# Attention steps of an HGRN2 and mixture-of-experts kernel: scores and Y in fours, the swapped v on GpSimd, banks allotted once, gate before the state products

## The chip, the cores and the metric

The kernel runs on one core of a Trainium2 chip. The core has five engines with their own instruction streams: TensorE (PE, with weight loads shown as PEld), VectorE (DVE), ScalarE (ACT), GpSimd (POOL) and SyncE (SP), which here issues transfers. They wait for each other by semaphores only. The metric is the time of one execution on the device in microseconds. The kernel before took 455.57 us (median of three runs, 452.97 to 456.45).

## The reference

Two blocks follow each other. The first is a gated linear recurrence for 4 batches and 8 heads, over 768 positions with a head width of 48:

```python
f = 1.0 / (1.0 + np.exp(-f_logit))
for t in range(S):
    state = f[:, :, t, :, None] * state + np.einsum('bhd,bhe->bhde', k[:, :, t], v[:, :, t])
    y[:, :, t] = np.einsum('bhd,bhde->bhe', q[:, :, t], state)
```

Its output, 3072 tokens of 384 values, goes to the second block: logits for 8 experts (`x @ w_gate`), an assignment of the tokens to the experts in order of their logits with at most 384 tokens per expert, and for each expert `max(x @ w1, 0) @ w2` with an inner width of 1024. All is float32.

## The kernel before, in words

**Tiling.** The recurrence is cut into chunks of 128 positions: 6 chunks of each of 4 batches, 24 in all, numbered so that the batch runs fastest. Within a chunk the recurrence becomes matrix products. With decays accumulated from the middle of the chunk (the rows up to 63 and those from 64 on have different signs), k and q are scaled by powers of the decay, and the scores k.q of all pairs of positions are formed, masked to the lower triangle, and multiplied by v. What comes from earlier chunks is added through a state per head, 48x48, which is carried from chunk to chunk of the same batch. The heads are packed in pairs on the partitions: a head's 48 rows are padded to 64, and a pair fills the 128.

**The stages of a chunk**, each a small function that takes a chunk's dictionary `G`:

- `load` and `fetch` (L140, L147): q, k, f and v come in by transfers of 192 KB from SP, f one chunk further ahead.
- `load_turned` (L156): two transfers of 64 KB each copy half of v inside the chip, so that the upper and lower 64 positions of heads 4 to 7 change places. The result is w.
- `clamp` (L162, GpSimd), `decays` (L166, ScalarE: exponential and logarithm), `cumulated` (L171, one matmul of float32, which is two passes on TensorE), `clipped` (L177, VectorE, from that sum's bank L), `powers` (L182, ScalarE: ek and eq), `scaled` (L187: kg on GpSimd, qg on VectorE).
- `turn_q`, `turn_k` and their copies (L229): four transposes each into a bank of PSUM, the accumulation memory of TensorE, and a copy by ScalarE.
- `lengths`, `spanned`, `faded`, `kept_part`, `products`, `next_state` (L201 to L267): the decay over the whole chunk and the state.
- `scores` (L269): 16 matmuls of 64x64 tiles, 128 or 64 columns wide; the array works as four tiles, two for the rows (`par`) and two for the output partitions. `masked0` and `masked1` (L281, VectorE) copy them under the mask out of the two banks A.
- `inner` (L300): 16 matmuls of masked scores with v (heads 0 to 3) and w (heads 4 to 7) into the two banks Y; `outer` (L314): 8 with the state.
- `joined` (L325): ScalarE copies one bank Y and VectorE adds the other. `turn_y`, `copy_y` (L331, L337) turn the sum to tokens in rows; `gate` (L344) forms the logits from it in 16 weight loads, into columns of bank L beside the decay sums; `gated`, `with_logits`, `store` (L353 to L361) put x and its logits into a table in HBM.

**The order.** Nothing is scheduled by a program: `tc.manual_schedule` (L611) keeps the order in which the Python code issues. `attention` (L386) runs through steps; in each it first issues `load_turned` and `load`, and then the tuple `stages` (L364), where each entry names a stage and how many chunks behind the step it works: (`scores`, 1) at step 10 is chunk 9. So every engine has a fixed order within a step, and several chunks are in work at once. `begun`, `drain` and `finale` are the orders of the first and last steps, and (None, 0) marks where small extra work (`later`, L380) goes, mainly on VectorE: tables for the second block, and from L573 the first choices of experts.

**Banks.** PSUM has eight banks: one L, two T (turns), two A, two Y and one small. A and Y are allotted once (L110). L is allotted anew in each step (`room[0] = L`, L172), and T anew for each turn of q, k and y in rotation (L231, L332), so three turns per step pass over two banks.

After the attention part come the counting and sorting of the assignment (L732 on) and the experts (`ffn`, L653), whose two large matmul lines are L674 and L688.

## Time and profile before

| what | value |
|---|---|
| median of three runs | 455.57 us |
| profiled execution, its own time | 453.23 us |
| span from first to last instruction | 451.4 us |
| mean granted TensorE clock | 0.978 |
| TensorE busy | 423.5 us, 94% |
| VectorE / ScalarE / GpSimd busy | 186.8 / 151.6 / 117.2 us |
| matmuls of the scores (L276), busy | 21.8 us with 128, 20.0 us with 64 columns |
| gate (L350) with mean of one | 13.0 us in the steps, 203 ns |
| SP issues of w (L159) | 48, 64 KB each, 2.6 us to landing |
| packets of the transfer queue | 119,664, 52.11 MB |

An instruction's line is that of the kernel's text, and a name such as `qg` is the tile that it writes or reads. "Idle before" is the time in which the engine had nothing to do ahead of an instruction, with what ended it. TensorE's matmuls are pipelined, so their durations overlap: the distance between starts tells more. The attention part reaches to about 157 us, the counting and sorting to about 178 us, and the experts to the end.

### The profile page before, as it was taken

How to read it: one execution, taken by the hardware profiler on the slowest of the kernel's cores; microseconds unless marked ns; L12 is line 12 of the kernel's file. 1: busy time of each engine (PE TensorE's matmuls, PEld its weight loads, DVE VectorE, ACT ScalarE, POOL GpSimd, SP SyncE). 2: the span in 40 equal slices, each digit the busy share in tenths (PEclk: the TensorE clock that was granted, in tenths of full speed). 3: DMA queues.
4: the chain of work that ended last, by engine and by line, in shares of the span. 5: the costliest groups of instructions: out<-in, count | busy, mean ns of one | idle time of the engine just before them, and what ended most of it. 6: DMA issues, size and time to landing. Idle time of an engine off the chain costs nothing.

```text
span 451.4 us, 11287 instructions
## 1 busy us (share of the span) xinstructions
PE 423.5 (94%) x4743; PEld 311.8 (69%) x4743; DVE 186.8 (41%) x600; ACT 151.6 (34%) x350; POOL 117.2 (26%) x182
## 2 busy tenths in 40 slices
PE   7789999999999768999999999999999999999991
PEld 3678887888787646767686868688887556556550
DVE  5679788777788763176565661000000000000000
ACT  4656565665665201222121213122323212213200
POOL 5344444334444006710100105111013203011010
PEclk9999999999999859999999999999999999999997
DMA  8888887987786792845353003048842201100000
GB/s 163 163 183 193 185 188 169 205 195 176 168 199 158 241 383 61 274 177 184 122 173 143 17 19 108 17 162 298 306 161 65 62 19 49 39 17 36 0 36 22
DMA packets 122987, 62.47 MB, mean 138 GB/s; under 512 B 103088, under 2 KB 117552, under 8 KB 122928
## 3 DMA queue, kind: packets, MB, share of 16 engines
q1 hardware_dynamic: 119664, 52.11, 43.3%
q0 software_dynamic: 3264, 9.56, 6.5%
q8 instruction: 39, 0.64, 0.6%
q14 instruction: 20, 0.16, 0.1%
HBM read 48.91 MB, written 9.54 MB: 129 GB/s over the span
## 4 chain that ended last, share of the span: by engine, by line
PE 65%; issue 13%; DMA 7%; DVE 5%; SPq 3%; ACT 3%; POOL 2%; POOLq 0%; ACTq 0%
PE H L674 22%; PE O L688 21%; DMA f<-in_f_logit_dram 4%; PE T L233 3%; DMA w<-v 3%; PE Y L309 3%; PE A L276 2%; PE nothing L106 2%; SPq L152 2%; PE X L334 2%; PE L L174 2%; PE Y L320 1%; PE small L254 1%; PE Xe L663 1%; POOL out_dram L694 1%
## 5 line engine op out<-in xcount | busy, mean ns | idle before, releaser
L688 PE MATMUL O<-w,hT 128*128 128x384 f32 x384 | 132.6, 490 | 0.0
L674 PE MATMUL H<-xeT,w 128*128 128x256 f32 (+2 forms) x624 | 130.6, 366 | 0.7 <-ACT xeT L666 0.7
L674 PEld LDWEIGHTS H<-xeT,w 128*128 128x128 f32 x624 | 99.1, 191 | 27.1 <-ACT xeT L666 1.0
L688 PEld LDWEIGHTS O<-w,hT 128*128 128x128 f32 x384 | 69.7, 190 | 39.2 <-issue 0.2
L694 POOL DMA_INDIRECT out_dram<-o,tok x24 | 23.5, 977 | 210.7 <-ACT o L693 201.1
L678 ACT ACTIVATE hT<-H 128x256 f32<-128x256 f32 (+2 forms) x104 | 38.2, 368 | 88.3 <-PE H L674 86.4
L693 ACT COPY o<-O 128x384 f32<-128x384 f32 x24 | 11.5, 479 | 74.5 <-PE O L688 73.0
L284 DVE COPY_PREDICATED am<-mask,A 128x512 f32<-128x512 int32 x48 | 34.4, 723 | 0.3 <-PE A L276 0.2
L666 ACT COPY xeT<-Xe 128x384 f32<-128x384 f32 x24 | 11.4, 480 | 61.4 <-PE Xe L663 61.4
L191 POOL TENSOR_TENSOR kg<-k,ek 128x384 f32<-128x384 f32 x24 | 26.1, 1087 | 12.9 <-ACT ek L185 12.6
L727 POOL DMA_INDIRECT xe<-xd,tok x24 | 23.3, 969 | 23.2 <-DMA w<-in_moe_w_dram 16.2
L191 DVE TENSOR_TENSOR qg<-q,eq 128x384 f32<-128x384 f32 x24 | 22.2, 926 | 12.8 <-ACT eq L185 12.7
L328 ACT COPY yT<-Y 128x512 f32<-128x512 f32 x24 | 14.1, 586 | 35.4 <-PE Y L320 31.2
L276 PE MATMUL A<-qT,kT 48*64 48x128 f32 (+1 forms) x768 | 21.8, 251 | 0.0
L309 PE MATMUL Y<-am,w 64*64 64x64 f32 (+1 forms) x384 | 19.6, 247 | 1.7 <-DMA w<-v 1.7
L233 PE MATMUL T<-ident,qg 128*128 128x128 f32 x96 | 15.7, 284 | 5.6 <-DVE qg L191 5.0
L163 POOL TENSOR_SCALAR f<-f 128x384 f32<-128x384 f32 x24 | 12.8, 533 | 31.2 <-DMA f<-in_f_logit_dram 31.2
L174 PE MATMUL L<-g,wcum 128*128 128x384 f32 x48 | 19.8, 494 | 0.6 <-ACT g L169 0.6
L329 DVE TENSOR_TENSOR yT<-Y,yT 128x512 f32<-128x512 f32 x24 | 16.4, 683 | 8.1 <-ACT yT L328 8.0
L309 PE MATMUL Y<-am,v 64*64 64x128 f32 (+1 forms) x384 | 19.5, 247 | 0.1
L276 PEld LDWEIGHTS A<-qT,kT 48*64 48x64 f32 x768 | 18.0, 133 | 0.5
L168 ACT ACTIVATE f<-f 128x384 f32<-128x384 f32 x24 | 12.7, 528 | 16.7 <-POOL f L163 16.7
(203 smaller groups left out, 520.4 us busy)
## 6 DMA issues: line engine op xcount, KB each, us to landing
w<-in_moe_w_dram SPq DMA_DIRECT2D x16, 1536.0 KB, 8.0
xd<-x SPq DMA_DIRECT2D x24, 196.0 KB, 3.6
f<-in_f_logit_dram SPq DMA_DIRECT2D x24, 192.0 KB, 4.1
k<-in_k_dram SPq DMA_DIRECT2D x24, 192.0 KB, 4.0
q<-in_q_dram SPq DMA_DIRECT2D x24, 192.0 KB, 3.8
v<-in_v_dram SPq DMA_DIRECT2D x24, 192.0 KB, 4.2
w<-v SPq DMA_DIRECT2D x48, 64.0 KB, 2.6
xe<-xd,tok POOLq DMA_INDIRECT x24, 3.2
```

What stands on the lines that cost most here:

```text
L174: nc.tensor.matmul(out=G["Lv"], lhsT=wcum[:], rhs=g_bufs[G["i"] % NB][:, :, 0:DH], start=True, stop=True)
L191: eng.tensor_tensor(out=t[:, :, 0:DH], in0=G[src][:], in1=G[e][:], op=ALU.mult)
L233: nc.tensor.transpose(out=T[:, 128 * hp:128 * hp + 128], in_=G[src][:, 2 * hp:2 * hp + 2, :].rearrange("t h d -> t (h d)"), identity=ident[:])
L276: nc.tensor.matmul(out=A[par][to, 128 * hp + first * j:128 * hp + 128], lhsT=G["kT"][rows, hp, HC * j:HC * j + HC], rhs=G["qT"][rows, hp, ...
L284: nc.vector.copy_predicated(am[:, par].rearrange("s (a b) t -> s a b t", b=2), mask[:].unsqueeze(2).to_broadcast((128, 2, 2, 128)), A[par] ...
L309: nc.tensor.matmul(out=G["Y"][r0][DP * r:DP * r + DP, 128 * blk + first:128 * blk + 128], lhsT=v, rhs=G["am"][rows, h % 2, h // 2, first:128],
L329: nc.vector.tensor_tensor(out=flat, in0=G["Y"][0][:], in1=flat, op=ALU.add)
L674: nc.tensor.matmul(out=L["H"][:, 0:w], lhsT=slots[e][0][:, d, 128 * ft:128 * ft + 128], rhs=xT[:, d, 0:w], start=(d == 0), stop=(d == DC - 1))
L678: nc.scalar.activation(out=hT[:, ft, 0:w], in_=L["H"][:, 0:w], func=AF.Relu)
L688: nc.tensor.matmul(out=L["O"][:, 0:D], lhsT=hT[:, ft, 128 * i:128 * i + 128], rhs=slots[e][1][:, ft, :], start=(ft == 0), stop=(ft == FC - 1))
L694: nc.gpsimd.indirect_dma_start(out=outs[next(tiles)][:, :], out_offset=bass.IndirectOffsetOnAxis(ap=token(e, first_block + i), axis=0), in ...
L727: nc.gpsimd.indirect_dma_start(out=t[:], out_offset=None, in_=xd[:, :], in_offset=bass.IndirectOffsetOnAxis(ap=token(e, i), axis=0))
```

## The change

Four parts are changed together.

- In `scores` and `inner` the loops are reordered. Before, the four blocks came in the order 0, 2, 1, 3, each with its wide and narrow matmuls one after the other. Now each run of four matmuls has the same width and goes to the four different tiles.
- `load_turned` becomes the stage `turned`: GpSimd copies the two halves of v itself, 64 partitions by 256 values each. It stands in the order behind `lengths` and ahead of `powers`, for chunk step - 1; in the drain behind `copy_k`. SP issues no transfers for w.
- The banks T and L are allotted once. q and y always use T[0], k uses T[1]; the gate writes `lengthy`. Two small turns of the bounds and the last chunk's `inner` use them too.
- In `stages`, `gate` and `gated` move directly behind `turn_y` and `copy_y`, ahead of `products` and `lengths`; `masked1` moves behind `clipped`; `spanned` and `next_state` move behind `scaled`. Besides, the first choices of experts, which were made in steps 18 and 19 for two columns of chunks each, are made column by column in steps 7 to 21.

```diff
@@ -100,14 +100,15 @@
     v_bufs = [kept([128, H, DP], FP32, f"v{i}") for i in range(NV)]
     wg_rows = kept([128, HP, E], FP32, "wg_rows")
 
-    def idle_turns(n, tag="T"):
-        nothing = ps("nothing", tag)
+    def idle_turns(n, tag=None):
+        nothing = ps("nothing", tag) if tag else T[0]
         for _ in range(n):
             nc.tensor.matmul(out=nothing[:, 0:3 * 128], lhsT=ones16[:], rhs=idle[:], start=True,
                              stop=True)
 
     small = ps("small", "small")
-    A, Y = ([ps(nm, nm) for _ in range(2)] for nm in "AY")
+    lengthy = ps("L", "L")
+    T, A, Y = ([ps(nm, nm) for _ in range(2)] for nm in "TAY")
 
     with tc.manual_schedule(engines=FIXED):
         nc.scalar.preload_act_table_set("natural_log_exp_and_others")
@@ -153,11 +154,11 @@
                 out=t[:, :, 0:DH], in_=src[b, :, C * c:C * c + C, :].rearrange("h t d -> t h d"))
             G[nm] = t
 
-    def load_turned(G):
+    def turned(G):
         G["w"] = w = work.tile([128, H // 2, DP], FP32, name="w", tag="w", bufs=4)
         for z in range(2):
-            nc.sync.dma_start(out=w[HC * z:HC * z + HC],
-                              in_=G["v"][HC - HC * z:C - HC * z, H // 2:H])
+            nc.gpsimd.tensor_copy(out=w[HC * z:HC * z + HC],
+                                  in_=G["v"][HC - HC * z:C - HC * z, H // 2:H])
 
     def clamp(G):
         nc.gpsimd.tensor_scalar(out=G["f"][:], in0=G["f"][:], scalar1=3.0e38, scalar2=-40.0,
@@ -169,8 +170,7 @@
         nc.scalar.activation(out=g[:, :, 0:DH], in_=f[:], func=AF.Ln, bias=1.0, scale=1.0)
 
     def cumulated(G):
-        room[0] = L = ps("L", "L")
-        G["Lv"] = L[:, 0:D].rearrange("t (h d) -> t h d", d=DH)
+        G["Lv"] = lengthy[:, 0:D].rearrange("t (h d) -> t h d", d=DH)
         nc.tensor.matmul(out=G["Lv"], lhsT=wcum[:], rhs=g_bufs[G["i"] % NB][:, :, 0:DH],
                          start=True, stop=True)
 
@@ -228,10 +226,10 @@
 
     def turn_of(nm, src):
         def turn(G):
-            G[nm + "_ps"] = T = ps("T", "T")
+            G[nm + "_ps"] = t = T[nm == "kT"]
             for hp in range(HP):
                 nc.tensor.transpose(
-                    out=T[:, 128 * hp:128 * hp + 128],
+                    out=t[:, 128 * hp:128 * hp + 128],
                     in_=G[src][:, 2 * hp:2 * hp + 2, :].rearrange("t h d -> t (h d)"),
                     identity=ident[:])
 
@@ -268,15 +266,14 @@
 
     def scores(G):
         first = 0 if G["i"] == 0 else HC
-        for hp in ORDER:
-            for j in range(2):
-                to = slice(HC * (j ^ (hp // 2)), HC * (j ^ (hp // 2)) + HC)
-                for par in range(2):
-                    rows = slice(DP * par, DP * par + DH)
-                    nc.tensor.matmul(
-                        out=A[par][to, 128 * hp + first * j:128 * hp + 128],
-                        lhsT=G["kT"][rows, hp, HC * j:HC * j + HC],
-                        rhs=G["qT"][rows, hp, first * j:128], start=True, stop=True)
+        for b, j, a in ((b, j, a) for b in range(2) for j in range(2) for a in range(2)):
+            hp, to = 2 * a + b, slice(HC * (j ^ a), HC * (j ^ a) + HC)
+            for par in range(2):
+                rows = slice(DP * par, DP * par + DH)
+                nc.tensor.matmul(
+                    out=A[par][to, 128 * hp + first * j:128 * hp + 128],
+                    lhsT=G["kT"][rows, hp, HC * j:HC * j + HC],
+                    rhs=G["qT"][rows, hp, first * j:128], start=True, stop=True)
 
     def masked(G, pars=(0, 1)):
         G["am"] = am = a_bufs[G["i"] % NB]
@@ -295,21 +292,18 @@
     def places(blk):
         return [(4 * (blk // 2) + 2 * r + blk % 2, r) for r in range(2)]
 
-    ORDER = [0, 2, 1, 3]
-
     def inner(G):
         last = G is chunks[-1]
-        G["Y"] = [ps("Y", "L"), ps("Y", "T")] if last else Y
-        for blk in ORDER:
-            for r0 in range(2):
-                j = r0 ^ (blk // 2)
-                rows, first = slice(HC * r0, HC * r0 + HC), 0 if last else HC * j
-                for h, r in places(blk):
-                    v = G["v"][rows, h, :] if blk < 2 else G["w"][rows, h - H // 2, :]
-                    nc.tensor.matmul(
-                        out=G["Y"][r0][DP * r:DP * r + DP, 128 * blk + first:128 * blk + 128],
-                        lhsT=v, rhs=G["am"][rows, h % 2, h // 2, first:128],
-                        start=(blk == ORDER[0]), stop=G["R"] is None, skip_group_check=True)
+        G["Y"] = [lengthy, T[1]] if last else Y
+        for b, j, a in ((b, j, a) for b in range(2) for j in range(2) for a in range(2)):
+            blk, r0 = 2 * a + b, j ^ a
+            rows, first = slice(HC * r0, HC * r0 + HC), 0 if last else HC * j
+            for h, r in places(blk):
+                v = G["v"][rows, h, :] if a == 0 else G["w"][rows, h - H // 2, :]
+                nc.tensor.matmul(
+                    out=G["Y"][r0][DP * r:DP * r + DP, 128 * blk + first:128 * blk + 128],
+                    lhsT=v, rhs=G["am"][rows, h % 2, h // 2, first:128],
+                    start=(b == 0 and j == 0), stop=G["R"] is None, skip_group_check=True)
 
     def outer(G):
         if G["R"] is None:
@@ -329,7 +323,7 @@
         nc.vector.tensor_tensor(out=flat, in0=G["Y"][0][:], in1=flat, op=ALU.add)
 
     def turn_y(G):
-        G["X"] = X = ps("X", "T")
+        G["X"] = X = T[0]
         for hp in range(HP):
             nc.tensor.transpose(out=X[:, 128 * hp:128 * hp + 128], in_=G["yT"][:, hp, :],
                                 identity=ident[:])
@@ -343,7 +337,7 @@
 
     def gate(G):
         G["lg"] = r = (part_of(G, 0, E) if G["i"] + 3 >= len(chunks)
-                        else room[0][:, D:D + E])
+                        else lengthy[:, D:D + E])
         for hp in range(HP):
             for j in range(2):
                 half = slice(HC * j, HC * j + HC)
@@ -361,14 +355,14 @@
         nc.sync.dma_start(out=xd[row:row + C, :], in_=G["x"][:])
 
     chunks = [{"b": b, "c": c, "i": c * B + b} for c in range(NCH) for b in range(B)]
-    stages = ((clamp, -1), (masked0, 2), (joined, 3), (masked1, 2), (turn_q, 1), (copy_q, 1), (turn_k, 1),
-              (copy_k, 1), (cumulated, 0), (clipped, 0), (turn_y, 3), (copy_y, 3), (decays, -1),
-              (products, 1), (lengths, 0), (spanned, 0), (next_state, 1), (powers, 0),
-              (scaled, 0), (faded, 0), (kept_part, 0), (None, 0), (gate, 3), (gated, 3),
-              (with_logits, 3), (scores, 1), (inner, 2), (outer, 2), (store, 3))
+    stages = ((clamp, -1), (masked0, 2), (joined, 3), (turn_q, 1), (copy_q, 1), (turn_k, 1),
+              (copy_k, 1), (cumulated, 0), (clipped, 0), (masked1, 2), (turn_y, 3), (copy_y, 3),
+              (gate, 3), (gated, 3), (decays, -1), (products, 1), (lengths, 0), (turned, 1),
+              (powers, 0), (scaled, 0), (spanned, 0), (next_state, 1), (faded, 0), (kept_part, 0),
+              (None, 0), (with_logits, 3), (scores, 1), (inner, 2), (outer, 2), (store, 3))
     begun = tuple(x for x in stages if x[1] >= 0) + ((clamp, -1), (decays, -1))
     drain = ((masked0, 2), (masked1, 2), (turn_q, 1), (joined, 3), (copy_q, 1), (turn_k, 1),
-             (copy_k, 1), (gate, 3), (gated, 3), (scores, 1), (None, 0), (turn_y, 3), (copy_y, 3),
+             (copy_k, 1), (turned, 1), (gate, 3), (gated, 3), (scores, 1), (None, 0), (turn_y, 3), (copy_y, 3),
              (inner, 2), (outer, 2), (masked0, 1), (masked1, 1), (None, 1), (with_logits, 3),
              (store, 3))
     finale = ((joined, 3), (inner, 2), (outer, 2), (None, 0), (gate, 3), (gated, 3), (turn_y, 3),
@@ -385,8 +379,6 @@
 
     def attention(first, last):
         for step in range(first, last):
-            if 0 <= step - 1 < len(chunks):
-                load_turned(chunks[step - 1])
             if AHEAD <= step + AHEAD < len(chunks):
                 load(chunks[step + AHEAD])
             order = stages
@@ -520,13 +512,13 @@
         ts(ends4[:, 0], ends4[:, 0], -1.0, ALU.mult)
         reduce(xs[:], ends4[:], ALU.max)
         yield
-        r = ps("ends", "T")
+        r = T[1]
         nc.tensor.transpose(out=r[0:2, 0:128], in_=xs[:], identity=ident[:])
         top, dg = rt([1], "top"), rt([2], "dg")
         reduce(top[0:2], r[0:2, 0:128], ALU.max)
         ts(dg[0:2], ident[0:2, 0:2], top[0:2], ALU.mult)
         yield
-        r = small[:, 416:418]
+        r = T[1][:, 0:2]
         nc.tensor.matmul(out=r, lhsT=onesf[0:2, :], rhs=dg[0:2], start=True, stop=True)
         two, width = rt([2], "two"), rt([1], "width")
         nc.vector.tensor_copy(out=two[:], in_=r)
@@ -570,10 +562,9 @@
     SEEN = 4
     LAST = len(chunks) - 1
     ranged = bounds(SEEN)
-    later(LAST - 5, lambda: first_choices(0, B, 0, 2))
-    later(LAST - 5, lambda: first_codes(0, B, 0, 2))
-    later(LAST - 4, lambda: first_choices(0, B, 2, SEEN))
-    later(LAST - 4, lambda: first_codes(0, B, 2, SEEN))
+    for c in range(SEEN):
+        later(B * c + B + 3, lambda c=c: first_choices(0, B, c, c + 1))
+        later(B * c + B + 5, lambda c=c: first_codes(0, B, c, c + 1))
     for i in range(3):
         later(LAST - 3 + i, lambda: next(ranged))
     END = NCH - 1
```

More of the change, by code (lines that the diff above doesn't have):

```diff
@@ L192, in scaled @@
             G[nm] = t
-    room = [None]
     def part_of(G, at, n):
```

## Prediction

> **What bounds the kernel now.** I read the slices of the page first (TensorE is busy in nine tenths of nearly every slice, but with two limits: an attention part up to about 157 us and an expert part behind it), then the chain of waits, then the timeline of single steps. The change touches the attention part alone; what follows it is taken over unchanged, so a microsecond saved per step is a microsecond of the span.
>
> The timeline of one step without disturbance (step 9 of the loop in `attention`), columns: start, duration, engine, line, operation, [idle before it, who ended it]:
>
> ```profile
> 55.79 0.42 PEld L233 LDWEIGHTS T<-ident,qg 128*128 128x128 f32 x4 [0.19 <-issue]
> ...
> 56.53 0.69 DVE L329 TENSOR_TENSOR yT<-Y,yT 128x512 f32<-128x512 f32 x1 [0.92 <-ACT yT L328]
> ...
> 56.73 0.81 PE L174 MATMUL L<-g,wcum 128*128 128x384 f32 x2
> ...
> 57.34 0.42 PEld L334 LDWEIGHTS X<-ident,yT 128*128 128x128 f32 x4 [0.42 <-ACT qT L241]
> ...
> 57.76 0.55 DVE L179 TENSOR_SCALAR dl<-L 128x384 f32<-128x384 f32 x1
> ...
> 57.92 0.55 PEld L254 LDWEIGHTS small<-v,kg 128*64 128x64 f32 x16 [0.17 <-DMA xd<-x]
> ...
> 58.85 0.55 PEld L350 LDWEIGHTS L<-wg_rows,yT 128*64 128x64 f32 x16
> ...
> 59.54 1.32 POOL L191 TENSOR_TENSOR kg<-k,ek 128x384 f32<-128x384 f32 x1
> ...
> 61.37 0.31 PEld L233 LDWEIGHTS T<-ident,qg 128*128 128x128 f32 x3 [0.18 <-issue]
> ```
>
> From one L233 to the next TensorE needs 5.58 us, and it idles once, 0.42 us before L334, until yT is there. The q turns of steps 7 and 21 start at 43.66 and 128.27 us, so the mean step between them is 84.61 / 14 = 6.04 us: 0.46 us more than the undisturbed one. Who ends these waits:
>
> ```profile
> PEld Y L309 <- DMA w<-v: 2.4, 4, 0.9
> ...
> PE Y L309 <- DMA w<-v: 1.7, 3, 0.7
> ```
> ```profile
> POOL f L163 <- DMA f<-in_f_logit_dram: 31.2, 21, 3.4
> POOL gl L214 <- DVE spans L211: 32.1, 19, 3.0
> ```
>
> The turned copy w arrives while TensorE stands in front of Y, and f arrives so late that GpSimd waits for it in nearly every step; behind f stand two activations on ScalarE and then ek and eq, so a late f delays qg and the next q turn. The issues on SP of one step show why:
>
> ```profile
> 86.19 1.11 SPq L159 DMA_DIRECT2D w<-v  x2
> 87.35 0.58 SPq L152 DMA_DIRECT2D q<-in_q_dram  x1
> 87.98 0.70 SPq L152 DMA_DIRECT2D k<-in_k_dram  x1
> 88.78 1.72 SPq L152 DMA_DIRECT2D f<-in_f_logit_dram  x1
> 90.54 0.63 SPq L152 DMA_DIRECT2D v<-in_v_dram  x1
> 91.27 0.64 SPq L361 DMA_DIRECT2D xd<-x  x1
> 92.01 1.11 SPq L159 DMA_DIRECT2D w<-v  x2
> ```
>
> SP issues without a pause, and one issue per step takes 1.7 us instead of 0.6. The store at 91.27 sends an x that was ready at 85.91: SP is a step behind, so transfers pace the loop, with TensorE close below. In the packets between 40 and 140 us the 192-byte loads are 78% of the DMA time, w 8.9%, the store 10%; the share is 0.84, or 5.1 us of work per step for each of 16 engines. About once in 5.4 us a 16 KB instruction packet holds one engine for about 1 us, during which the data packets of the others run dry. 5.1 + 1.0 is the step that is measured.
>
> **What the Trainium skill says.** "TensorEngine Tiling (Array Packing)", Key Properties: different tiles load and multiply in parallel, and a change of tiling mode drains the engine. The trace agrees: 0.17 to 0.19 us idle before L233 and L254, and four 64*64 tiles running at once. "SBUF — State Buffer", Who interferes with whom: a VectorE instruction with two SBUF inputs and a GpSimd instruction that reads SBUF exclude each other for the whole instruction; one with a single SBUF input does not contend. The trace agrees: qg takes 0.57 us when it starts before kg (kg then 1.32) and 1.05 when kg starts first (kg then 1.00); clamp beside dl costs neither anything. "GPSIMD Engine Reference", Engine selection: one-input operations run roughly at line rate; L163 with 533 ns for 384 elements and L357 with 188 ns for 8 agree.
>
> **Part by part.** *Fours.* In the scores of the step at 92.07 us one of the four 64*64 tiles starts its passes at 95.70, 95.86, 95.97, 96.03, 96.09, 96.20, 96.31 and 96.36 us (a matmul of this type is two passes): after the first, 109 ns for a pass of 128 columns and 56 to 59 for one of 64, without a hole. With 4 of each a tile needs 4 x 109 + 4 x 56 = 660 ns in either order; the block takes 0.63 us from its first weight load to Y's, and Y 0.67. Equal lengths save only the uneven end, and Y loses its two DMA waits: I take 0.04 us together. Bounds: 0.4 us gained, if all 64 passes went at the 14 ns at which bursts of ten start (64 x 14 = 0.9 of 1.3 us), to 0.1 lost for a slower first four.
>
> *w on GpSimd.* Removed per step: two issues (1.11 us of SP's 6.0) and 8.9% of the DMA time, 0.45 us per engine, more than what the loop lacks. So the 0.46 us of disturbance go. Added: two copies of 64x256. The two rows above give 0.92 ns per element over 0.18 us: 0.42 us each, 0.84 together. Bounds 0.25 (half the partitions, half the time) to 0.75 us each (the two-input rate of L191, 1087 ns for 384, scaled). They stand behind clamp and in front of kg. Clamp ends at 0.9 us in the step, the copies at 1.8, ek not before 3.17, so kg waits for nothing new; if f came later than 2 us into the step, kg would slip. Sum on GpSimd: 0.53 + 0.84 + 1.09 + 0.20 + 0.72 + 0.19 = 3.6 of 5.9 us. spanned moves behind scaled, so kg no longer stands behind gl (which waited 32.1 us in all): kg starts at 3.2 instead of 3.75, but then qg, ready at 3.58, is the one that is held (1.05). It ends at 4.6, k at 4.2, both before the next turn at 5.9: nothing.
>
> *Gate in front.* L350 moves from behind 32 weight loads (L254, L206) to directly behind L334. It writes the bank that dl reads, and the program waits there for dl. dl needs L: the second matmul of L174 ends 1.74 us into the step, an idle VectorE starts dl 0.04 later (so at 10.8 and 15.9 us) and takes 0.56: 2.34, and TensorE follows 0.12 later (as X follows yT), 2.46. X frees TensorE at 2.13 (where L254 starts now). So a new hole of 0.33 us per step, where before dl was done 0.5 us ahead of L350. Queued behind it: products, lengths, scores, Y, all of TensorE. VectorE in turn idles 0.35 us before dl, since masked1 now stands behind dl; with qg held its loop comes to about 4.9 us plus 0.3 to 1.0 of extras, so it stays under 5.9 in most steps. Bounds: 0 (another wait is longer) to 0.4 us.
>
> *Banks, routing.* Turn banks by name drop TensorE's waits on its own earlier turns, and L no longer waits for gated (which stood behind the extras and cost 0.2 us in steps 19 and 20): within the 0.04 above. The first choices go from steps 18 and 19 to eight odd steps, 0.36 us of VectorE each, hidden; steps 19 and 20 took 6.30 and 6.26 us and lose their excess, already counted in the mean.
>
> **Sum**, against the profiled execution (453.2 us, span 451.4). Step: 5.58 + 0.33 - 0.04 = 5.87, say 5.85. Steps 7 to 20: 14 x (6.04 - 5.85) = 2.7. Steps 21 to 23, without products (0.47 less): 17.37 before, 3 x 5.38 + 0.4 for the bounds' turns = 16.5 after, 0.9. Steps 1 to 6: step 4 took 6.53 where its work gives 5.6, mostly for a late f; steps 3 and 5 pay the hole; 0.9 together. Total 4.5, or 448.7. The median of the three runs (455.6) lies 2.4 above that execution; I subtract from the median: 451.1.
>
> **Rivals.** *TensorE goes faster than the tiles' sum* (fours at 0.2 us less, half the bound, or no hole): 14 x 0.2 + 1 more, 447.5. For it: bursts of starts 7 ns apart; against: no hole in a tile. *Transfers still pace it*: the instruction packets stay, and what an engine stalls on is a packet, not bytes; step 6.0, 454.5. For it: the late landings follow these packets; against: 5 issues instead of 7. *GpSimd becomes the bound*, the slower side: the copies cross partition halves, which no row shows. Its other work is 2.7 us; at 2.0 us a copy the step is 6.7, 17 x 0.68 = 11.5 more, 467. It decides from 6.31 us a step, so 1.8 us a copy. Against: four times the row's rate.
>
> **Chances.** Forecast 0.50, TensorE faster 0.23, transfers 0.14, GpSimd as the bound 0.13. Within 1% (4.6 us) a measurement of this kernel can't tell from no change, and my forecast lies at that edge. So faster is 0.23 + 0.25 = 0.48, same 0.25 + 0.14 and 0.02 of the last case, slower 0.11. Range: 446 (the full gain of the second case, 1.5 below its time) to 457 (half the slower cases).
>
> **What would show it.** L350 preceded by 0.3 us ended by DVE dl; no wait for w; SP's issues all near 0.6 us, stores within 2 us of their x; copies of 0.4 us on GpSimd; L233 to L233 5.85. I am wrong if steps stay at 6.0, if L350 starts at 2.15 into the step, or if scores take under 0.55 us.

## The result and the profile after

The changed kernel takes 452.1 us (median of 20 runs, 450.7 to 455.2) against 454.9 us of the kernel before: a ratio of 0.9948 with a 95% interval of 0.9925 to 0.9972, or 2.4 us less (1.3 to 3.4). The forecast was 4.5 us less, 451.1. The profiled execution of the changed kernel took 454.26 us at a span of 452.5, so it is one of its longer ones; this has to be kept in mind when it is laid beside that of before (453.23, span 451.4).

The timeline of one undisturbed step (step 11), columns as in the prediction:

```profile
67.66 0.42 PEld L231 LDWEIGHTS T<-ident,qg 128*128 128x128 f32 x4 [0.18 <-issue]
...
68.39 0.83 POOL L160 COPY w<-v 64x256 f32<-64x256 f32 x2
...
69.22 0.42 PEld L328 LDWEIGHTS T<-ident,yT 128*128 128x128 f32 x4 [0.44 <-ACT qT L239]
...
69.44 0.56 DVE L179 TENSOR_SCALAR dl<-L 128x384 f32<-128x384 f32 x1 [0.33 <-PE L L174]
...
70.05 0.55 PEld L344 LDWEIGHTS L<-wg_rows,yT 128*64 128x64 f32 x16 [0.41 <-DVE dl L179]
...
70.96 1.00 POOL L191 TENSOR_TENSOR kg<-k,ek 128x384 f32<-128x384 f32 x1 [1.74 <-issue]
...
71.26 1.11 DVE L191 TENSOR_TENSOR qg<-q,eq 128x384 f32<-128x384 f32 x1
...
73.48 0.20 PEld L231 LDWEIGHTS T<-ident,qg 128*128 128x128 f32 x2 [0.18 <-issue]
```

From one q turn to the next 5.82 us. The gate (L344) is behind the turn of y (L328), TensorE stands 0.41 us in front of it, and dl, which VectorE ends at 70.00, releases it. The two copies of w take 0.83 us right behind clamp; kg starts 3.30 us into the step and holds qg, which takes 1.11.

SP's issues in the same step, columns start, duration, queue, line, operation:

```profile
67.88 0.36 SPq L355 DMA_DIRECT2D xd<-x  x1
68.29 0.60 SPq L153 DMA_DIRECT2D q<-in_q_dram  x1
68.94 0.65 SPq L153 DMA_DIRECT2D k<-in_k_dram  x1
69.69 0.72 SPq L153 DMA_DIRECT2D f<-in_f_logit_dram  x1
70.51 0.65 SPq L153 DMA_DIRECT2D v<-in_v_dram  x1
73.75 0.36 SPq L355 DMA_DIRECT2D xd<-x  x1
```

None takes 1.7 us here (between 42 and 131 us three issues still take over 1.4 us; before there were eleven), SP pauses 2.6 us in front of the last, and that store follows 0.02 us behind the copy of the logits which completes its x. The list of waits (total, times, longest):

```profile
POOL gl L212 <- DVE spans L209: 10.8, 19, 0.6
...
PEld L L344 <- DVE dl L179: 9.1, 21, 0.9
...
PEld Y L303 <- issue: 4.1, 5, 1.3
...
POOL f L164 <- DMA f<-in_f_logit_dram: 4.0, 4, 2.3
...
PE Y L303 <- issue: 3.3, 4, 1.2
```

The wait for w is gone, and that for f is down from 31.2 us to 4.0. But in front of Y stands something else: "issue", time in which TensorE waits for nothing that the profile shows. One of these places in the timeline of weight loads:

```profile
102.83 0.13 PEld L303 LDWEIGHTS Y<-am,v 64*64 64x64 f32 x1
104.06 0.13 PEld L303 LDWEIGHTS Y<-am,v 64*64 64x64 f32 x2 [1.09 <-issue]
```

In the midst of the 32 passes of Y, with no wait between them, TensorE stops for 1.1 us. Five such gaps of 0.55 to 1.38 us lie in steps 7, 8 and 15 to 17. The step lengths from the starts of the q turns: 5.82 or 5.83 us in steps 9 to 14, 19 and 20, but 6.48, 7.05, 6.80, 7.00, 8.18 and 6.42 in steps 7, 8 and 15 to 18. Steps 7 to 20 together take 88.53 us where fourteen undisturbed ones would take 81.6, and the prediction had 81.9. Step 17 loses 1.0 us more than its gap of 1.38, and step 18 loses 0.6 us without a gap: from 110.81 to 114.22 us the granted clock of TensorE is 0.50 in this trace, and 1.00 in the rest of these steps.

The spans of all profiled executions, cut at the starts of the q turns of steps 7, 21 and 24 (the turns that begin these steps), in us. The kernels below "changed" are explained under Experiments. "Excess" is steps 7 to 20 less fourteen undisturbed steps. "Gaps" is the part of it in pauses over 0.2 us at the places that the next section names, and "half clock" is how long the granted clock was 0.50 within these steps:

| kernel | undisturbed step | up to step 7 | steps 7 to 20 | excess | gaps | half clock | steps 21 to 23 | the rest |
|---|---|---|---|---|---|---|---|---|
| before | 5.58 | 43.66 | 84.61 | 6.5 | 0.7 | 0 | 17.37 | 305.8 |
| changed | 5.83 | 42.49 | 88.53 | 6.9 | 5.2 | 3.4 | 16.58 | 304.9 |
| w alone | 5.59 | 42.39 | 84.49 | 6.2 | 5.3 | 0 | 16.49 | 305.2 |
| gate late | 5.59 | 42.64 | 85.37 | 7.1 | 5.1 | 3.4 | 16.39 | 304.8 |
| gate in small | 5.59 | 41.78 | 85.25 | 7.0 | 5.1 | 3.4 | 16.22 | 305.0 |
| fewer loads | 5.83 | 43.66 | 82.07 | 0.5 | 0.3 | 0 | 16.59 | |
| fours undone | 5.83 | 42.78 | 85.81 | 4.2 | 3.5 | 0 | 16.60 | 304.7 |
| w sent too | 5.83 | 44.54 | 85.22 | 3.6 | 2.8 | 0 | 17.00 | 304.8 |
| gate alone | 5.83 | 45.10 | 86.32 | 4.7 | 3.5 | 0 | 16.93 | 304.7 |
| lean | 5.96 | 41.92 | 85.31 | 1.9 | 1.6 | 0 | 16.89 | 304.7 |
| changed, second time | 5.83 | 43.78 | 85.97 | 4.4 | 4.1 | 0 | 16.59 | 317.6 |
| fours undone, second time | 5.83 | 43.54 | 85.81 | 4.2 | 3.4 | 0 | 16.60 | 317.0 |
| fours alone | 5.59 | 45.33 | 86.26 | 8.0 | 3.8 | 3.4 | 16.74 | 319.8 |
| gate in small, second time | 5.59 | 42.98 | 84.97 | 6.7 | 4.8 | 3.4 | 16.21 | 318.7 |

The rows from "w alone" to "fewer loads" ran in one group, beside runs of the kernel before, and those from "fours undone" to "lean" in another. The last four rows are from another chip, on which everything behind attention takes some 12 us longer; the first row's partner there is "fours alone", as shown below.

The clock tells the two traces of the changed kernel apart: third from the right is its mean between 42 and 131 us, in the first trace and in the second.

```profile
42.00:131.00 89.00, 82.54 (x1996) 69.11 (x1994) 67.88 (x163) 50.65 (x112) 43.63 (x99) 0.98 0.78 165
...
42.00:131.00 89.00, 83.50 (x2054) 69.80 (x2046) 69.49 (x167) 51.85 (x116) 45.30 (x104) 1.00 0.80 167
```

In the five traces that have it, the two steps that hold it lose 1.6 to 1.7 us beyond their gaps. It begins inside a gap of 1.0 to 1.4 us or at most 0.5 us behind one. Whether such a gap brings it about is not shown: "w alone" has two gaps of 1.4 us in these steps and no half clock.

### The profile page after: what moved, and what is told of

Its sections match the earlier page's. It is cut to its first block, busy times and chain, and to the rows that moved or that the text cites. A ratio compares the mean times of both kernels' runs of the same rounds, so it can differ in the third digit from the quotient of the medians.

```text
span 452.5 us, 11264 instructions
## 1 busy us (share of the span) xinstructions
PE 423.2 (94%) x4743; PEld 311.6 (69%) x4743; DVE 187.5 (41%) x608; ACT 151.4 (33%) x350; POOL 129.6 (29%) x230
## 4 chain that ended last, share of the span: by engine, by line
PE 72%; issue 15%; DVE 6%; POOL 3%; ACT 1%; POOLq 0%; ACTq 0%
PE H L665 22%; PE O L679 21%; PE T L231 5%; PE A L273 4%; PE Y L303 4%; PE L L174 3%; PE L L344 3%; DVE dl L179 3%; PE Y L314 2%; PE small L204 2%; PE small L252 2%; PE Xe L654 1%; POOL out_dram L685 1%; PE nothing L106 1%; PE cnt L778 1%
## 5 line engine op out<-in xcount | busy, mean ns | idle before, releaser
L191 POOL TENSOR_TENSOR kg<-k,ek 128x384 f32<-128x384 f32 x24 | 24.1, 1003 | 47.3 <-issue 46.9
L191 DVE TENSOR_TENSOR qg<-q,eq 128x384 f32<-128x384 f32 x24 | 26.4, 1101 | 4.7 <-ACT eq L185 2.6
L303 PE MATMUL Y<-am,v 64*64 64x128 f32 (+1 forms) x368 | 21.0, 247 | 2.4 <-issue 2.4
L303 PE MATMUL Y<-am,w 64*64 64x128 f32 (+1 forms) x368 | 20.7, 249 | 0.9 <-issue 0.9
L303 PEld LDWEIGHTS Y<-am,v 64*64 64x64 f32 x368 | 18.4, 136 | 2.6 <-issue 2.6
L160 POOL COPY w<-v 64x256 f32<-64x256 f32 x48 | 18.9, 394 | 2.5
L303 PEld LDWEIGHTS Y<-am,w 64*64 64x64 f32 x368 | 17.6, 136 | 1.5 <-issue 1.5
```

The lines of the kernel that those rows point to most:

```text
L160: nc.gpsimd.tensor_copy(out=w[HC * z:HC * z + HC], in_=G["v"][HC - HC * z:C - HC * z, H // 2:H])
L191: eng.tensor_tensor(out=t[:, :, 0:DH], in0=G[src][:], in1=G[e][:], op=ALU.mult)
L303: nc.tensor.matmul(out=G["Y"][r0][DP * r:DP * r + DP, 128 * blk + first:128 * blk + 128], lhsT=v, rhs=G["am"][rows, h % 2, h // 2, first:128],
```

## What stops TensorE

The gaps have no wait, so the question was what else TensorE can lack. I numbered all records of TensorE in the order of their starts: weight loads, matmuls, and the semaphore instruction that stands in front of the turn of y in each step (285 records a step in the changed kernel). The gaps of the changed kernel stand in front of numbers 1729, 1985, 4033, 4289 and 4545: every difference is a multiple of 256. The trace also has 16 KB instruction packets, one for about every 256 of these records, so 64 bytes each. For some of these boundaries, from the packet records of the trace (times in us):

```
changed kernel
boundary  boundary before  packet    packet   boundary  gap
number    passed at        starts    landed   passed    there
2753      66.06            67.56     68.49    71.56     0.00
3265      76.89            77.63     78.72    82.29     0.01
4033      91.58            94.64     95.81    97.36     0.99
4289      97.36            101.69    102.68   104.06    1.12
4545      104.06           108.73    109.67   111.05    1.38
4801      111.05           112.70    113.62   118.05    0.00

fewer loads
4033      91.39            93.59     94.61    96.18     0.00
4289      96.18            96.94     98.01    101.68    0.00
4545      101.68           102.38    103.33   107.26    0.00
```

With few loads most packets start 0.05 to 0.8 us after TensorE has passed the boundary before; in steps 7 to 20 of the changed kernel 0.4 to 4.7 us after it. A packet takes about 1.0 us, and where TensorE stands and waits, it goes on 1.4 to 1.6 us after the landing. Ahead of 4033 lie 4.8 us of work since the boundary before, and 5.6 us ahead of 4289 and 4545. So the packet may start about 4.8 - 1.2 - 1.6 = 2.0 us late for the first, and 5.6 - 1.0 - 1.4 = 3.2 us for the other two. They started 3.07, 4.33 and 4.67 us late, and what is over comes to about the gaps. The DMA engines are all busy meanwhile: their mean busy share (about 1 when all are) is 1.05 from 97.86 us to the start of the packet of 4289, and 0.07 from its landing to the end of the gap; 1.03 and 0.07 for 4545. This is the theory for the experiments: TensorE runs out of instructions, because the packets that bring them stand behind the data packets. No record shows when a packet is asked for. Its rivals: an accident of one execution; or a pause that has nothing to do with transfers.

The kernel before had it too, without my seeing it: at 1217, 1729 and 1985 its packets started 3.50, 3.05 and 3.33 us after the boundary before, and TensorE has gaps of 0.55, 0.33 and 0.33 us there, without a wait. The one at 1729:

```profile
48.80 0.14 PEld L309 LDWEIGHTS Y<-am,v 64*64 64x64 f32 x2 [0.31 <-issue]
```

## Experiments

**One part alone: w on GpSimd.** The kernel before, with load_turned replaced (its call is gone, and `turned` stands in the drain too):

```diff
-            nc.sync.dma_start(out=w[HC * z:HC * z + HC],
-                              in_=G["v"][HC - HC * z:C - HC * z, H // 2:H])
+            nc.gpsimd.tensor_copy(out=w[HC * z:HC * z + HC],
+                                  in_=G["v"][HC - HC * z:C - HC * z, H // 2:H])
...
-              (products, 1), (lengths, 0), (spanned, 0), (next_state, 1), (powers, 0),
+              (products, 1), (lengths, 0), (turned, 1), (spanned, 0), (next_state, 1), (powers, 0),
```

> The kernel before with one part of the change alone: GpSimd makes w, behind the lengths, and SP no longer sends it; fours, banks, gate and routing stay as before. Theory (w's two issues and transfers cost the loop 0.46 us a step; the gate's wait for dl costs the changed kernel 0.25 us a step, so this version has an undisturbed step of 5.58 us): 454.9 - 14 x 0.46 - 2 = 446 to 447 us if nothing new takes the place of the disturbance, and 449 to 450 if about as many unwaited TensorE stalls of 1 us appear as in the changed kernel's trace (six between 42 and 131 us). Rival (transfers still pace the loop, whatever w does): 453 to 455, with steps of 6.0 us. No wait for w, f at GpSimd within 0.5 us in both.

Measured: 450.7 us, ratio 0.9928 (0.9906 to 0.9951), 3.3 us less. The wait for w is gone, and what replaces it is seen in its timeline:

```profile
78.24 0.42 PEld L233 LDWEIGHTS T<-ident,qg 128*128 128x128 f32 x4 [0.18 <-issue]
...
83.83 0.42 PEld L233 LDWEIGHTS T<-ident,qg 128*128 128x128 f32 x4 [0.19 <-issue]
...
96.15 0.14 PEld L309 LDWEIGHTS Y<-am,v 64*64 64x64 f32 x2 [0.85 <-issue]
...
97.07 0.42 PEld L233 LDWEIGHTS T<-ident,qg 128*128 128x128 f32 x4 [0.19 <-issue]
...
102.98 0.14 PEld L309 LDWEIGHTS Y<-am,v 64*64 64x64 f32 x2 [1.40 <-issue]
```

An undisturbed step takes 5.59 us, as before, and there are more of them; but steps 7 to 20 take 84.49 us in all, and 84.61 before. What w and f cost there is gone, and late instructions took about as much: gaps of 5.3 us in this trace, 0.7 in that of before. In these traces its gain lies ahead of step 7 (1.3 us) and in steps 21 to 23 (0.9), where the loads run out.

**The gate put back, and the gate without its wait.** First the gate and gated of the changed kernel behind the lengths again; then the gate where the change puts it, but with its sums in the bank small, so that nothing makes it wait for dl:

```diff
 gate late
-              (gate, 3), (gated, 3), (decays, -1), (products, 1), (lengths, 0), (turned, 1),
+              (decays, -1), (products, 1), (lengths, 0), (turned, 1),
...
-              (None, 0), (with_logits, 3), (scores, 1), (inner, 2), (outer, 2), (store, 3))
+              (None, 0), (gate, 3), (gated, 3), (with_logits, 3), (scores, 1), (inner, 2), (outer, 2), (store, 3))
 gate in small
-        G["lg"] = r = (part_of(G, 0, E) if G["i"] + 3 >= len(chunks)
-                        else lengthy[:, D:D + E])
+        G["lg"] = r = part_of(G, 0, E)
...
-              (gate, 3), (gated, 3), (decays, -1), (products, 1), (lengths, 0), (turned, 1),
-              (powers, 0), (scaled, 0), (spanned, 0), (next_state, 1), (faded, 0), (kept_part, 0),
+              (gate, 3), (decays, -1), (products, 1), (lengths, 0), (turned, 1),
+              (powers, 0), (scaled, 0), (spanned, 0), (next_state, 1), (gated, 3), (faded, 0), (kept_part, 0),
```

> The changed kernel with gate and gated back behind the lengths and the state products, nothing else moved. Theory (the gate in front costs TensorE the 0.44 us hole that dl ends, 0.25 us more than the switch of tiles): undisturbed step 5.56 instead of 5.83 us, 17 steps, 447 to 448 us. Rival (what TensorE saves is given back by its unwaited stalls, since its instructions come in no faster): undisturbed steps of 5.56 but more stalls, 451 to 453 in all.

> The changed kernel with the gate where the change puts it, in front of the state products, but its sums in the bank small in every step, so that it has no wait for dl (gated is moved behind the new state, because the state products would else wait for it). Theory (the hole is the wait for dl in the shared bank, not the place of the gate): the idle time ahead of the gate falls from 0.44 to about 0.18 us, step 5.56, 447 to 448 us as with the gate behind. Rival (the place itself costs, for instance by another switch of tiles): step 5.7 or more, 450 to 452.

Measured: gate late 450.4 us, ratio 0.9909 (0.9884 to 0.9934); gate in small 450.0 us, ratio 0.9895 (0.9868 to 0.9921). The timeline of gate in small:

```profile
62.19 0.42 PEld L328 LDWEIGHTS T<-ident,yT 128*128 128x128 f32 x4 [0.44 <-ACT qT L239]
...
62.77 0.55 PEld L343 LDWEIGHTS small<-wg_rows,yT 128*64 128x64 f32 x16 [0.17 <-issue]
...
63.23 0.55 PEld L252 LDWEIGHTS small<-v,kg 128*64 128x64 f32 x16
```

The gate in front now has 0.17 us ahead of it instead of 0.41, the state products behind it none, and the undisturbed step is 5.59 instead of 5.83. So the place costs nothing; the wait for dl in the shared bank costs 0.24 us a step. Both kernels miss the 447 to 448 us that this alone would give, and why is not shown: their excess in steps 7 to 20 is 7.1 and 7.0 us (some 5.1 in gaps, 1.6 at the half clock), about that of the changed kernel in its first trace, and more than the 4.4 of its second.

**Transfers taken away.** Three of four loads left out (in steps 5 to 21), f loaded as ever:

```diff
         for nm, src in parts:
+            if G["i"] > 6 and nm == "v":
+                G[nm] = v_bufs[G["i"] % NV]
+                continue
+            if G["i"] > 4 and nm in "qk":
+                G[nm] = chunks[G["i"] % 5][nm]
+                continue
```

> The changed kernel without the loads of q and k from the sixth chunk on and of v from the eighth on: the tiles loaded before are used again, f is loaded as ever. Three of four loads are left out in steps 5 to 21; TensorE's work and waits stay. Theory (the unwaited TensorE stalls of the changed kernel are late instruction fetches, held up by the data packets): no unwaited gap over 0.5 us in scores, Y and the R products, every step 5.83 us, 446 to 448 us. Rival 1 (these stalls have nothing to do with transfers): as many stalls of 1 us as in the changed kernel, 451 to 453. Rival 2 (they are an accident of the one profiled execution): no stalls but also no gain, 452.

Measured: the kernel leaves out loads, so the expert part gets other values from attention, and what follows attention takes 8 ms. The total (8305 us) answers nothing, and only attention is read here. Its q turns:

```profile
90.78 0.42 PEld L237 LDWEIGHTS T<-ident,qg 128*128 128x128 f32 x4 [0.19 <-issue]
...
96.60 0.42 PEld L237 LDWEIGHTS T<-ident,qg 128*128 128x128 f32 x4 [0.18 <-issue]
...
102.43 0.42 PEld L237 LDWEIGHTS T<-ident,qg 128*128 128x128 f32 x4 [0.18 <-issue]
...
108.25 0.20 PEld L237 LDWEIGHTS T<-ident,qg 128*128 128x128 f32 x2 [0.18 <-DVE code L423]
```

These are the steps that took 6.80, 7.00 and 8.18 us in the changed kernel; here they take 5.82 or 5.83, with the wait for dl in each. Steps 7 to 20 take 82.07 us, where fourteen steps of the forecast make 81.9. Rival 1 falls: the share of busy DMA engines between 42 and 131 us goes from 0.78 to 0.28, and the gaps of steps 15 to 17 go with it. That the packets wait behind data packets is read from the packet table, not from a view of a queue. In steps 6 to 8 the packets still start 2.7 to 3.6 us late, with gaps of 0.49 us at 1473 and 0.30 at 1985. There, too, they start as a run of data packets ends: the DMA engines' busy share is 0.84, 0.74 and 0.94 in the microsecond before the packets of 1473, 1729 and 1985 start, and 0.02, 0.10 and 0.12 in the one after.

The late packets of the changed kernel come in two groups, before 1473 to 1985 and before 4033 to 4545, 2560 records apart. Ten packets are 2560 records and nine steps are 2565. So after nine steps the boundaries lie at nearly the same place of a step again, here in Y, and meet the same transfers.

**Transfers added.** The changed kernel with the two transfers of w beside its copies, into a tile that nobody reads:

```diff
+    def sent(G):
+        w = work.tile([128, H // 2, DP], FP32, name="sent", tag="sent", bufs=4)
+        for z in range(2):
+            nc.sync.dma_start(out=w[HC * z:HC * z + HC],
+                              in_=G["v"][HC - HC * z:C - HC * z, H // 2:H])
...
+            if 0 <= step - 1 < len(chunks):
+                sent(chunks[step - 1])
```

> The changed kernel, whose w comes from GpSimd, with the two transfers of the kernel before beside it: they go from v into a tile that nobody reads. Theory (the data packets delay TensorE's instruction packets, and SP's issues delay f): with the 0.45 us of transfers per step back, but no wait for them, the loop falls behind again at f and at unwaited TensorE stalls, 453 to 456 us. Rival (all that w cost was TensorE's wait for w): 452, as the changed kernel.

Measured: 453.0 us, ratio 0.9986 (0.9961 to 1.0010). Beside the 0.9948 of the changed kernel it looks as if the gain were gone, though no engine waits for these transfers. But the two ratios come from two groups of runs, and in this run's group "fours undone", which is level with the changed kernel on one chip further down, stands at 1.0028. So it is not shown that these transfers cost time. What the trace shows are its SP issues and, from its list of waits, GpSimd's wait for f:

```profile
82.19 1.12 SPq L166 DMA_DIRECT2D sent<-v  x2
83.35 0.59 SPq L153 DMA_DIRECT2D q<-in_q_dram  x1
83.98 0.60 SPq L153 DMA_DIRECT2D k<-in_k_dram  x1
84.69 1.72 SPq L153 DMA_DIRECT2D f<-in_f_logit_dram  x1
```
```profile
POOL f L170 <- DMA f<-in_f_logit_dram: 15.7, 15, 2.9
```

Long issues are back (eleven over 1.4 us between 42 and 131 us), and f is late again (15.7 us, and 4.0 in the changed kernel). It reaches step 7 2.05 us later, but TensorE also has a granted clock of 0.50 from 25.33 to 28.75 us in this trace, which the changed kernel's has not; what each cost is not separated. In steps 7 to 20 it has fewer unwaited gaps, not more (2.8 us): I expected more of both, and only the late f came. So more data packets do not in themselves make the instruction packets later, and the theory does not say what else decides.

**The places alone.** The kernel before with the gate and gated in front of the products and masked1 behind dl, w still sent:

```diff
-    stages = ((clamp, -1), (masked0, 2), (joined, 3), (masked1, 2), (turn_q, 1), (copy_q, 1), (turn_k, 1),
-              (copy_k, 1), (cumulated, 0), (clipped, 0), (turn_y, 3), (copy_y, 3), (decays, -1),
-              (products, 1), (lengths, 0), (spanned, 0), (next_state, 1), (powers, 0),
-              (scaled, 0), (faded, 0), (kept_part, 0), (None, 0), (gate, 3), (gated, 3),
-              (with_logits, 3), (scores, 1), (inner, 2), (outer, 2), (store, 3))
+    stages = ((clamp, -1), (masked0, 2), (joined, 3), (turn_q, 1), (copy_q, 1), (turn_k, 1),
+              (copy_k, 1), (cumulated, 0), (clipped, 0), (masked1, 2), (turn_y, 3), (copy_y, 3),
+              (gate, 3), (gated, 3), (decays, -1), (products, 1), (lengths, 0),
+              (spanned, 0), (next_state, 1), (powers, 0), (scaled, 0), (faded, 0), (kept_part, 0),
+              (None, 0), (with_logits, 3), (scores, 1), (inner, 2), (outer, 2), (store, 3))
```

> The kernel before with the places of the change alone (gate and gated in front of the products, masked1 behind dl); w still sent by SP. Theory (the hole for dl is 0.25 us a step on TensorE's path, but the loop of the kernel before is held at 6.04 us by w and f and takes up most of it): 454 to 456.5 us, mean step 6.05 to 6.15. Rival (the hole adds in full): 454.1 + 17 x 0.25 = 458.3.

Measured: 454.5 us, ratio 1.0011 (0.9975 to 1.0048). Its undisturbed step is 5.83 us, 0.25 more than before, and the time shows nothing of it that can be told from no change. The interval ends at 2.2 us more, and 17 x 0.25 would be 4.3: the loop, held up elsewhere, absorbs at least half, as expected.

**Fewer TensorE instructions.** Gate in small, with the lengths as four products of 128*128 between L and the turn of y:

```diff
-            for r in range(2):
-                nc.tensor.matmul(out=ends[DP * r:DP * r + DP, :, hp], lhsT=g[:, 2 * hp + r, :],
-                                 rhs=ind[:], start=True, stop=True)
+            nc.tensor.matmul(out=ends[:, :, hp],
+                             lhsT=g[:, 2 * hp:2 * hp + 2, :].rearrange("t h d -> t (h d)"),
+                             rhs=ind[:], start=True, stop=True)
...
-              (copy_k, 1), (cumulated, 0), (clipped, 0), (masked1, 2), (turn_y, 3), (copy_y, 3),
+              (copy_k, 1), (cumulated, 0), (lengths, 0), (clipped, 0), (masked1, 2), (turn_y, 3), (copy_y, 3),
...
-              (gate, 3), (decays, -1), (products, 1), (lengths, 0), (turned, 1),
+              (gate, 3), (decays, -1), (products, 1), (turned, 1),
```

> The version with the gate's sums in the bank small, and the lengths made by four 128*128 products between L and the turn of y, where TensorE idles 0.44 us for yT, in place of eight 128*64 ones behind the state products: 16 of some 257 TensorE instructions less per step. Theory (TensorE is limited by its own work and by its instructions' arrival, both of which this shortens): undisturbed step 5.2 to 5.4 instead of 5.59 us; 445 to 448 us, with stalls left because the instructions are asked for as fast as before. Rival 1 (eight loads of 128x128 take longer than sixteen of 128x64): step 5.6 or more, 450 or more. Rival 2 (another engine's loop, VectorE with 4.9 us and extras, or the transfers are next): step 5.5, 449 to 450.

Measured: 451.7 us, ratio 0.9989 (0.9961 to 1.0018). Rival 1 holds; from its timeline:

```profile
72.98 1.18 PEld L203 LDWEIGHTS small<-ind,g 128*128 128x128 f32 x8
...
74.00 0.51 PEld L328 LDWEIGHTS T<-ident,yT 128*128 128x128 f32 x4
```

Eight loads of 128x128 hold TensorE from 72.98 to 74.00, 1.02 us or 128 ns each, where sixteen of 128x64 take 0.46 to 0.47; the step is 5.96 us. Yet steps 7 to 20 take 85.31 us, about as much as gate in small with steps of 5.59: its gaps are 1.6 us instead of 5.1, and it has no half clock there. Its gaps stand at 3777, 4033 and 4289, again on the grid of 256, though a step now has 269 records instead of 285 (the expectation's 257 is a miscount): the grid belongs to the instruction stream and not to scores or Y. With 269 records it takes twenty steps until the boundaries lie at the same place again, and there is one group of gaps in these steps, not two.

**The fours.** The changed kernel with the old order of scores and Y (the loops over ORDER put back, as in the diff of the change), run in two groups; the changed kernel itself again in the second; and the kernel before with the new order alone.

> The changed kernel with scores and Y in the order of the kernel before (128 and 64 columns in turn), all else as changed. Theory (a tile's passes leave no hole in either order, so the fours are worth at most 0.04 us a step): undisturbed step 5.82 to 5.87 us, 452 to 453 us, scores and Y 0.66 and 0.67 us. Rival (the fours save 0.2 us or more a step): step above 6.0 us, 455 us or more.

> The changed kernel once more, as the measure for the three beside it. Theory (its unwaited TensorE stalls lie at fixed places of the instruction stream, every 256 instructions, where the instructions come late): a second trace has them at the same instructions 1729, 1985, 4033, 4289 and 4545 of TensorE's stream, with 5.83 us in the steps without one; 452 us. Rival (the stalls were an accident of one execution): other places or none.

> The changed kernel with the order of the kernel before in scores and Y, now beside the changed kernel on one chip. Its undisturbed step was the same 5.83 us, but its median lay 2 us above. Theory (the order changes nothing in a step; what differs is chance in the stalls and between chips): within 1 us of the changed kernel's median. Rival (the order decides how long the stalls last, which stand in scores and Y): 2 us or more above it.

> The kernel before with the fours alone. Theory (0.04 us a step at most, and the loop is held by w and f): within 1 us of the kernel before, ratio 0.998 to 1.002. Rival (the order decides how long stalls last): 2 us or more faster, ratio below 0.996.

> The version with the gate in front and its sums in the bank small, now beside the changed kernel on one chip. Theory (it saves the 0.25 us hole in each of 17 steps, less what the stalls give back): 2 to 3 us below the changed kernel, ratio 0.988 to 0.991 to the kernel before. Rival (the stalls give all of it back): within 1 us of the changed kernel.

Measured first: 454.3 us, ratio 1.0028 (1.0004 to 1.0052) for fours undone, which beside the 0.9948 of the changed kernel looked like 3 to 4 us for the fours, with the same 5.83 us in every undisturbed step. Those two ratios came from two groups of runs. In one group on one chip, all beside 469.7 us of the kernel before: changed kernel 0.9909 (0.9876 to 0.9941), fours undone 0.9922 (0.9900 to 0.9943), fours alone 1.0000 (0.9975 to 1.0025), gate in small 0.9863 (0.9825 to 0.9901). So the fours are worth nothing that can be measured, and that difference was not theirs. The changed kernel has its gaps at 1729, 1985, 4033 and 4545 a second time (at 4289 only 0.3 us), so they are no accident:

```profile
111.23 0.13 PEld L303 LDWEIGHTS Y<-am,v 64*64 64x64 f32 x1 [1.30 <-issue]
```

Fours alone shows that the kernel before starves as well, where w happens to be in time; its waits between 40 and 132 us:

```profile
PEld Y L305 <- issue: 3.4, 4, 1.4
...
PEld Y L305 <- DMA w<-v: 1.3, 1, 1.3
```

Gate in small has the lowest median in both groups in which it ran: 1.1 and 1.4% under the kernel before, and 1.9 us under the changed kernel on one chip, where six runs of each leave their intervals overlapping. That is about half of the 17 x 0.24 = 4.1 us which its step saves. In the two traces of that chip its gaps are 0.7 us longer than the changed kernel's, and of the two it alone has a half clock; what keeps the other half in general is not shown.

## Why the prediction was right, and where it was not

The time lay in the range and 1.0 us above the forecast, but that is in part luck: the saving was 2.4 us (1.3 to 3.4) instead of 4.5, and the forecast was subtracted from a median of three that lay 0.7 us above the later one of twenty. In the sum two of three terms came out, and the largest did not.

*Fours, 0.04 us a step.* Right: 5.83 us with either order, 0.9909 against 0.9922 on one chip, 1.0000 alone. The scores take 0.66 us and Y 0.67, as the tiles' passes add up.

*w on GpSimd.* The prices are right: copies of 394 ns on average (forecast 0.42), kg 3.3 us into the step (3.2), qg held at 1.11 (1.05), no wait for w; in the step shown SP's issues at 0.36 to 0.72 us and the store right behind its x. GpSimd is far from being the bound.

*Gate in front.* Right in kind and place: TensorE waits for dl in the bank L. The hole is 0.41 us, 0.17 of which is the switch of tiles that stood there anyway; 0.24 us net, forecast 0.33. With that the undisturbed step is 5.83 (forecast 5.85).

*The sum.* Steps 1 to 6 came out: 1.2 us less in the profiled pair (forecast 0.9). Steps 21 to 23 as well: 0.8 (0.9). The term that failed is "Steps 7 to 20: 14 x (6.04 - 5.85) = 2.7". It took for granted that the 0.46 us by which the mean step exceeded the undisturbed one were w's and f's, and would go with them. They went, but something took their place: over these steps TensorE loses 5.2 and 4.1 us in gaps in the two traces of the changed kernel, and 5.3 with w alone, which has no w to wait for. The first trace loses another 1.6 us at the half clock. The mean step is 6.32 and 6.14 us, above the 6.04 of before. Without the half clock, steps 7 to 20 take some 86.9 and 86.0 us in the changed kernel, and 84.6 both in the kernel before and in fours alone, which is as fast. So in these traces the middle lost 1.4 to 2.3 us where 2.7 were to be gained. The two terms that came out are 2.0 us in the profiled pair. That they make up the 2.4 us measured is not shown: single executions differ by more than that, and this pair as a whole is 1.0 us slower.

The rival that said "transfers still pace it, instruction packets stay" (step 6.0, 454.5) had the middle of the loop about right in its number, but not in its reason (the other rival's 447.5 is 447.3 by its own sum). It had data packets coming late behind the instruction packets, and the prediction says that they run dry during one. The packet records of before do not bear that out: the share of data packets is 0.84 during the instruction packets between 42 and 131 us, and 0.83 over the whole. The packet table speaks for the other way round. The prediction looked at the 16 KB packets only as a hindrance for data; that TensorE itself needs one for every 256 records, and about every 5.5 us, was not asked. The sign to look for was in the trace of before: gaps of 0.33 and 0.55 us without a wait, inside Y and inside a q turn.

## What to carry to other kernels

When a profile shows an engine stopped with no wait in the midst of equal instructions, number its instructions: gaps at a fixed spacing suggest that the instructions themselves are late. While such a supply is near its limit, a microsecond taken from each step can be partly given back (here about half was missing), and one added can be partly free, so undisturbed steps must not be multiplied by their number. Look at the granted clock of each stretch, too, before two traces are laid side by side: here a half clock of 3.4 us made 1.6 us of difference between two executions of one kernel. And a difference between two groups of runs, each set against its own runs of the kernel before, is to be measured again within one.

## What the runs showed of the hardware

- TensorE's instructions come in 16 KB packets, one for every 256 of its records. With little else to move most start 0.05 to 0.8 us after the boundary before is passed; in the loaded loop up to 4.7 us. In the changed kernel's first trace it is 1.38 to 1.59 us from the landing to the next instruction of a waiting TensorE.
- The gaps of steps 7 to 20 are shorter in all where the step is longer, though the ranges overlap: 4.8 to 5.3 us at steps of 5.59 without w's transfers (0.7 and 3.8 with them), 2.8 to 5.2 at 5.83, 1.6 at 5.96, where a step also has 16 records fewer.
- In five of fourteen traces TensorE's granted clock is 0.50 for 3.4 us within steps 7 to 20; the two steps that hold it lose 1.6 to 1.7 us beyond their gaps.
- Sixteen weight loads of 128x64 pass in 0.46 to 0.47 us, eight of 128x128 with two moving columns each in 1.02.
- A copy of 64x256 across the halves of the partitions takes GpSimd 394 ns.
